# Fourier mixing and gated convolution FFN on one core: the tables loaded by halves of x, first halves of the products during the loading

## The chip, the cores and the metric

The kernel runs on one core of a Trainium2 chip. The core has five engines with instruction streams of their own: TensorE (PE, with PEld for its weight loads), VectorE (DVE), ScalarE (ACT), GpSimd (POOL) and SyncE (SP), and 16 DMA engines that serve all queues of the core. The metric is device time in microseconds (us), the median of several runs; less is better.

## The reference

`x` has 8 batches of 3136 rows and 256 features. The kernel computes the real part of a two-dimensional Fourier transform over rows and features and feeds it to a gated FFN with a convolution over the rows (`d_ff` 1024, three taps).

```python
X = np.fft.fft(x, axis=1)
X = np.fft.fft(X, axis=2)
x = X.real.astype(np.float32)
h = np.maximum(x @ w_in, 0.0)
...
for k in range(K):
    conv_out += conv_w[k][None, None, :] * hp[:, k:k + S, :]
gate = 1.0 / (1.0 + np.exp(-conv_out))
return (h * gate @ w_out).astype(np.float32)
```

## The kernel before

The transform is folded by its symmetries. Rows of x that mirror each other, and features that mirror each other, are added and subtracted on DVE (`fold_ops`, L142 to 237), so that a batch becomes two weight tiles `w`: `wt[b][0]` for the even rows of the spectrum and `wt[b][1]` for the odd ones, each with four sums (with the cosine and the sine of the features) for four residues `q` of the row. A batch is loaded in two tiles `xh[b, h]` (`load_ops`, L110 to 140): one plain DMA of 98 partitions for the lower rows, four indirect DMAs by GpSimd for the mirrored ones, and for the half `h = 1` three DMAs that bring row 0 into partition 98. Half `h` serves the residues `q = 2h` and `q = 2h + 1` of every weight tile. A tile that is loaded with `held` is first touched by a memset of GpSimd (L118), behind the issue of the loads before it.

PE multiplies the weight tiles with tables of cosines and sines (`tabs`, L242): `tab2` holds the even table (sine or cosine, four residues `q`, 393 columns each), `tab4` the odd one (four variants, of which ACT makes two from the other two, `mirror_tables`, L298; 196 columns). `load_even` (L256) brings `tab2` in four DMAs: even and odd partitions up to 95, two more rows, and the row of partition 98; `load_odd` (L270) brings one variant of `tab4` in three or four. `mend_row` (L292) scales the table rows of partitions 96 and 97. For batch 0 the odd weight tile is also scaled by `turn` factors on ACT (`scaled`, L211, operation L218), a half at a time, into tiles `h`.

The products of a batch are nine units (`Unit`, L305): `odd_even(1)`, `odd(1)`, `even_even(1)`, `even(1)`, `feature()`, then `odd_even(0)`, `odd(0)`, `even_even(0)`, `even(0)`. The argument says cosine or sine. `odd` and `odd_even` give the odd columns of the results, `even` and `even_even` the even ones; the products of `odd` and of both even units read `tab2`, those of `odd_even` read `tab4`. Each unit fills one PSUM bank by matmuls (all through `mm`, L93), ACT copies a part of the bank (`copy`) and DVE makes sums and differences of it (`fin`) that end in the result tiles `pt` (cosine) and `qt` (sine), tile `PQ[b]`. `feature` gives the row `er` of one single feature, by ten sums on GpSimd and `flip` on ACT (L460).

The main loop takes a batch in 32 steps (4 chunks of rows times 8 blocks of `d_ff`). A step makes its first product from `pt`, `qt` and the matrix `G` (`products`, L781 and L782): first `pb` from `qt`, then `pa` from `pt`, the latter on top of a seed that ACT writes from `eb` (the broadcast of `er`) and `ge` (L769). `G` and `ge` come from `w_in` and the transform matrix `dm` of the features: `blocks(i)` (L735, one fourth of the columns, four matmuls of 256 columns, two copies of ACT) and `column(i)` (L746). The weights `w_in` and `w_out` arrive as 64-bit floats and are made 32-bit by DVE (`narrow`, L606 to 639, the first step at L620). Everything else of the loop overlaps: while the steps of one batch run, the units of the next one are laid between them at fixed places. The order within each engine is the order of the program (`manual_schedule`, L66).

The change touches the start, before the first step. There the order of the program is: load of the taps (ACT's queue) and of `w_in[0]` (SP), x of batch 0 (first half on SP and GpSimd, `turn` on ACT's queue, second half on SP and GpSimd with its zero rows on ACT's queue), first use of the sigmoid (L717, which loads ACT's table of functions), narrowing of the taps and of `w_in[0]`, `taps` (L696), three memsets of GpSimd at L722 to 724 that the table loads wait for, the tables, `dm`, the other three fourths of `w_in`. Then come all folds of batch 0 (L885 to 889), eight matmuls whose result nobody reads (`keep_on`, L875, on `wt[0][1]`), mending and mirroring of the tables on ACT, and the four odd units by quarters (L898 to 908):

```python
for i in range(4):
    for j, u in enumerate(odds):
        u.part(i)
        if i == 3:
            u.copy()
            u.fin()
```

After them the units `feature`, `even_even(1)`, `even(1)`, `even_even(0)`, `even(0)` run one after the other (L910), then the broadcast of `er` by a matmul with `one` (L921), `column(0)`, the load of x's next half, `blocks(0)`, the narrowing of `w_in[1]` (L929), and the steps.

Of the kernel before, what the change touches and what calls it, by code (L numbers as in the profile page):

```python
# [9 lines left out]
F32 = mybir.dt.float32  # L10
# [27 lines left out]
def kernel(  # L38
# [71 lines left out]
    def load_ops(b, h, eng, other=None, held=False):  # L110


        def plain():
            t = xp.tile([P, 8, 2, D], F32, name="xh", tag="xh")
            xh[b, h] = t
            if held:

                nc.gpsimd.memset(t[0:1, 0, 0, 0:1], 0.0)  # L118
# [137 lines left out]
    def load_even():  # L256

        to = tabs[0].rearrange("p s q i -> p s (q i)")
        n = HQ * HE
        for i in range(2):  # L260
            nc.sync.dma_start(out=to[i:2 * MR:2], in_=dft_seq[0:MR, 0:2, HQ * i:HQ * (i + 1)]
                              .rearrange("p s q i -> p s (q i)"))
        nc.sync.dma_start(out=to[2 * MR:NP], in_=bass.AP(
            tensor=dft_seq.tensor, offset=dft_seq.offset + MR * 4 * NQ * HE,
            ap=[[n, 2], [NQ * HE, 2], [1, n]]))
        nc.sync.dma_start(out=to[NP:KR], in_=bass.AP(
            tensor=dft_seq.tensor, offset=dft_seq.offset + (NP * 4 * NQ - HQ + 2) * HE,
            ap=[[n, 1], [NQ * HE, 2], [1, n]]))

    def load_odd(eng, s):  # L270

        def at_(p, q):
            return dft_seq.offset + ((p * 4 + 2 + s) * NQ + q) * HE
        for i in range(2):
            eng.dma_start(out=tabs[1][i:2 * MR:2, s], in_=bass.AP(
                tensor=dft_seq.tensor, offset=at_(0, HQ * i + 1), ap=[[4 * NQ * HE, MR], [2 * HE, 2], [1, QO]]))
        eng.dma_start(out=tabs[1][2 * MR:NP, s], in_=bass.AP(
            tensor=dft_seq.tensor, offset=at_(MR, 1), ap=[[HQ * HE, 2], [2 * HE, 2], [1, QO]]))
        if s:
            eng.dma_start(out=tabs[1][NP:KR, 0:2, 1], in_=bass.AP(  # L280
                tensor=dft_seq.tensor, offset=dft_seq.offset + ((NP * 4 + 2) * NQ + 1) * HE,
                ap=[[HE, 1], [NQ * HE, 2], [1, QO]]))
# [15 lines left out]
    def mirror_tables():  # L298

        for to, of, s in ((2, 1, -1.0), (3, 0, 1.0)):  # L300
            for i in range(2):
                act(tabs[1][0:KR, to, :, i:QO:2], tabs[1][0:KR, of, :, i:QO:2], AF.Copy,
                    scale=-s if i else s)

    class Unit:  # L305
# [31 lines left out]
    def units(b):  # L337
# [5 lines left out]
        def even_even(sn):  # L343
# [3 lines left out]
                           True, True) for j, q in ((0, 3), (1, 1)) for c in range(2)]  # L347
# [42 lines left out]
        def odd(sn):  # L390
# [16 lines left out]
            def fin(p):  # L407
# [301 lines left out]
    w_cv.load(nc.scalar)  # L709
    w_in[0].load(nc.sync)  # L710
# [414 lines left out]
```

## Time and profile before

| | |
|---|---|
| median of 3 runs | 1173.87 us (1173.63 to 1175.4) |
| profiled execution | 1175.2 us; span 1173.4 us, granted clock 0.998 |
| PE busy | 1139.6 us (97%), 4818 matmul records |
| PEld, DVE, ACT, POOL busy | 887.5, 970.7, 942.9, 606.9 us (76, 83, 80, 52%) |
| DMA | 168.15 MB, mean 143 GB/s |
| chain that ended last | PE 77%, ACT 4%, DVE 3% |

Times in views of the profile are in us from the start of the span. A row of a timeline gives start, duration, engine, line, operation, result and operands with partitions and elements, the number of instructions (xcount), and in brackets the idle time ahead of it with what released it. SPq and ACTq are the queues' issuing instructions on those engines. q0 is the DMA queue that GpSimd fills, q1 the one of SP and ACT; their rows give packets, MB and the share of the 16 DMA engines' time in the window.

### The profile page before, as it was taken

What the parts mean: (1) busy time and instruction counts of PE and PEld (TensorE: products, weight loads), DVE (VectorE), ACT (ScalarE), POOL (GpSimd) and SP (SyncE); (2) the same over time, 40 slices, a digit from 0 to 9 for tenths busy, and PEclk for the clock granted to TensorE, in tenths of its full rate; (3) what the DMA queues carried; (4) which work ended last, traced back from release to release, by engine and by line L of the source; (5) the groups of instructions that cost most, each with busy time, mean ns of one, the idle gap of its engine ahead of it and who ended that gap; (6) DMA issues with size and microseconds to landing.
All of it is one profiled execution on the core that took longest, in us unless ns stands there. A gap on an engine that the chain in (4) does not pass through costs nothing.

```text
span 1173.4 us, 15901 instructions
## 1 busy us (share of the span) xinstructions
PE 1139.6 (97%) x4818; PEld 887.5 (76%) x4818; DVE 970.7 (83%) x1448; ACT 942.9 (80%) x1939; POOL 606.9 (52%) x734
## 2 busy tenths in 40 slices
PE   4889999999999999999999999999999999999998
PEld 2756777778778777777777777777778777777777
DVE  7589979998788789798886888889787778788885
ACT  2578868888788888888887878888887888898885
POOL 5346755666465554756455464654344344444443
PEclk9999999999999999999999999999999999999999
DMA  8777787776677676667676676865665656666654
GB/s 209 192 108 156 165 138 165 160 162 135 141 159 168 136 169 141 147 135 176 144 166 139 122 149 141 177 126 121 135 120 107 126 122 142 130 130 129 126 116 102
DMA packets 106050, 168.15 MB, mean 143 GB/s; under 512 B 31121, under 2 KB 61091, under 8 KB 105965
## 3 DMA queue, kind: packets, MB, share of 16 engines
q0 software_dynamic: 41984, 115.83, 51.7%
q1 hardware_dynamic: 62809, 50.88, 15.8%
q8 instruction: 38, 0.62, 0.2%
q10 hardware_dynamic: 1172, 0.43, 0.2%
q14 instruction: 47, 0.39, 0.1%
HBM read 38.40 MB, written 25.74 MB: 55 GB/s over the span
## 4 chain that ended last, share of the span: by engine, by line
PE 77%; ACT 4%; DVE 3%; issue 1%; DMA 0%; POOL 0%; ACTq 0%; DVEq 0%
PE po L93 49%; PE pb L93 12%; PE pa L93 11%; PE pd L93 6%; ACT nb L790 1%; DVE g L813 1%; ACT os L861 1%; ACT g L828 1%; DMA out_dram<-os 0%; ACT pa L769 0%; DVE g L837 0%; DVE w L228 0%; DVE xh L168 0%; ACT g L804 0%; DVE pt L418 0%
## 5 line engine op out<-in xcount | busy, mean ns | idle before, releaser
L93 PE MATMUL po<-wout,g 128*128 128x256 f32 x3072 | 708.3, 380 | 6.6 <-DVE g L837 5.8
L93 PEld LDWEIGHTS po<-wout,g 128*128 128x128 f32 x3072 | 581.6, 190 | 152.5 <-issue 19.7
L808 POOL DMA_DIRECT2D g<-h x256 | 227.7, 889 | 464.5 <-ACT g L804 270.6
L828 ACT ACTIVATE g<-g,cw 128x385 f32<-128x385 f32 (+2 forms) x512 | 292.3, 625 | 68.1 <-DVE g L813 65.5
L836 POOL TENSOR_TENSOR g<-g,h 128x385 f32<-128x385 f32 (+1 forms) x256 | 301.2, 1177 | 49.5 <-ACT g L828 47.9
L790 ACT ACTIVATE nb<-pb 128x386 f32<-128x386 f32 (+3 forms) x512 | 227.3, 499 | 112.1 <-PE pb L93 111.4
L798 DVE CUSTOM_DVE_ANT_0 h<-pa,nb 128x386 f32<-128x386 f32 (+3 forms) x512 | 264.3, 556 | 29.3 <-POOL h L775 19.8
L813 DVE SCALAR_TENSOR_TENSOR g<-h,cw,g 128x770 f32<-128x770 f32 (+1 forms) x256 | 282.8, 1105 | 0.0
L804 ACT ACTIVATE g<-h,cw 128x770 f32<-128x770 f32 (+1 forms) x256 | 244.4, 955 | 0.0
L93 PE MATMUL pb<-qt,G 127*128 127x387 f32 (+2 forms) x512 | 214.0, 499 | 2.6 <-ACT nb L790 1.1
L93 PE MATMUL pa<-pt,G 128*128 128x387 f32 (+2 forms) x512 | 212.3, 495 | 1.2 <-ACT pa L769 1.2
L837 DVE TENSOR_TENSOR g<-g,h 128x385 f32<-128x385 f32 (+1 forms) x256 | 187.0, 730 | 25.0 <-ACT g L828 24.8
L769 ACT ACTIVATE pa<-eb,ge 128x387 f32<-128x387 f32 (+2 forms) x256 | 155.4, 607 | 1.3 <-DVE h L798 1.0
L93 PEld LDWEIGHTS pa<-pt,G 128*128 128x128 f32 x512 | 96.4, 189 | 76.4 <-issue 17.4
L132 POOL DMA_INDIRECT xh<-in_x_dram,idx x64 | 91.1, 1423 | 18.5 <-issue 12.2
L93 PE MATMUL pd<-tab,w 98*128 98x197 f32 (+2 forms) x448 | 98.0, 318 | 0.8 <-DVE w L228 0.7
L93 PEld LDWEIGHTS pb<-qt,G 127*128 127x128 f32 x512 | 90.8, 190 | 9.7 <-ACT nb L790 2.7
L93 PEld LDWEIGHTS pd<-tab,w 98*128 98x128 f32 (+1 forms) x448 | 81.8, 191 | 10.5 <-DVE w L228 1.0
L861 ACT COPY os<-po 128x256 f32<-128x256 f32 x196 | 57.4, 395 | 6.5 <-PE po L93 6.5
L168 DVE TENSOR_TENSOR xh<-xh 98x1024 f32<-98x1024 f32 (+1 forms) x32 | 47.4, 1482 | 0.1
L157 DVE TENSOR_TENSOR xh<-xh 98x1020 f32<-98x1020 f32 (+1 forms) x32 | 46.9, 1471 | 0.0
L385 DVE TENSOR_TENSOR as<-as,pd 128x196 f32<-128x196 f32 x14 | 5.0, 358 | 38.0 <-ACT as L381 38.0
(140 smaller groups left out, 447.7 us busy)
## 6 DMA issues: line engine op xcount, KB each, us to landing
g<-h POOLq DMA_DIRECT2D x192, 385.0 KB, 4.1
g<-h POOLq DMA_DIRECT2D x64, 416.0 KB, 4.4
out_dram<-os SPq DMA_DIRECT2D x96, 256.0 KB
xh<-in_x_dram SPq DMA_DIRECT2D x16, 784.0 KB
eb<-ed SPq DMA_DIRECT2D x16, 193.5 KB
raw<-in_moe_w_in_dram SPq DMA_DIRECT2D x4, 512.0 KB
raw<-in_moe_w_out_dram SPq DMA_DIRECT2D x1, 2048.0 KB
eb<-ed SPq DMA_DIRECT2D x8, 209.0 KB
```

Of the source, the lines that this page charges most:

```text
L93: nc.tensor.matmul(o, l, r, start=start, stop=stop, skip_group_check=True)
L132: nc.gpsimd.indirect_dma_start(out=xh[b, h][0:NP, 7 - m].rearrange("p q d -> p (q d)"), out_offset=None, in_=bass.AP(tensor=x.tensor, offs ...
L769: act(pa[s][:, 0:n], eb[b, c], AF.Copy, scale=ge[:, f:f + 1])
L790: act(nb[s][:, i, cols], p[:, cols], AF.Copy, scale=-1.0 if i else 1.0)
L798: nc.vector._custom_dve(TENSOR_ADD_SAT, out=to, in0=a[:, cols], in1=c[:, i, cols], s0=BIG, s1=0.0)
L804: act(gs[s], hs[s][:, 0:n], AF.Copy, scale=cw[:, 0, s[2]:s[2] + 1])
L808: nc.gpsimd.dma_start(out=gs[s], in_=hs[s][:, 1:1 + n], accum_op=ALU.add)
L813: stt(out=g, in0=h[:, k:k + n], scalar=cw[:, k, f:f + 1], in1=g, op0=ALU.mult, op1=ALU.add)
L828: act(gs[s][:, c], gs[s][:, c], AF.Sigmoid, scale=cw[:, 1, s[2]:s[2] + 1])
L836: gt(g[:, p], g[:, p], h[:, p], op=ALU.mult)
L837: vt(g[:, v], g[:, v], h[:, v], op=ALU.mult)
L861: nc.scalar.copy(out=osb[:, j % 2], in_=pt[:, j % 2])
```

## The change

- **Tables by halves.** `load_tables(eng, h)` brings what half `h` of x needs: 590 columns (393 of residue 2h and 197 of residue 2h + 1) of each of the two rows of `tab2`, even and odd partitions in a DMA each, and the residue's part of the two loaded variants of `tab4`, two DMAs. Of the columns left out of the load, ACT makes those of the cosines from the others (`mirror_cosines`); those of the sines are not read. The rows of partitions 96 to 98 are loaded by `rest_even`, `rest_odd` and `last_row`.
- **Queues and order.** The first half's tables are issued on SP behind x's first half; x's second half is issued by GpSimd, plain DMA and indirect ones, its zero rows by SP among the tables; `dm` stands between the tables of the two halves. The rows of partitions 96 and 97 go by ACT's queue early. The first use of the sigmoid comes right behind the load of the taps. The `held` memset and two of the three memsets ahead of the tables are gone.
- **First halves.** `part` takes halves of a unit's matmuls. `even_even` and `even` are reordered so that their first half reads residues of half 0. Between the folds of half 0 and those of half 1 the program now has the first halves of the four odd units and of three of the four small even units, `blocks(0)` (both of its pieces in one bank) and `column(0)`; they stand ahead of the mending and mirroring of half 1, of its folds and of the second halves. In the main loop blocks and columns stay.
- **The matmuls that nobody reads** are ten on the taps `cw24` instead of eight on `w`; two more of 118 and 119 columns stand behind the second halves of the first two even units.
- **GpSimd takes two sums** of batch 0: those of `odd(0)` into `pt`.

```diff
-    def load_ops(b, h, eng, other=None, held=False):
+    def load_ops(b, h, eng, other=None):
...
+    HM = HO // 2 + 1
+
+    def load_tables(eng, h):
+
+        to = tabs[0].rearrange("p s q i -> p s (q i)")
+        q0, n = 2 * h * HE, HE + HM
+        for i in range(2):
+            eng.dma_start(out=to[i:2 * MR:2, :, q0:q0 + n], in_=bass.AP(
+                tensor=dft_seq.tensor, offset=dft_seq.offset + HQ * i * HE + q0,
+                ap=[[4 * NQ * HE, MR], [NQ * HE, 2], [1, n]]))
+        for i in range(2):
+            eng.dma_start(out=tabs[1][i:2 * MR:2, 0:2, h], in_=bass.AP(
+                tensor=dft_seq.tensor, offset=dft_seq.offset + (2 * NQ + HQ * i + 2 * h + 1) * HE,
+                ap=[[4 * NQ * HE, MR], [NQ * HE, 2], [1, QO]]))
+
...
-    def mirror_tables():
-
+    def mirror_tables(h):
+
+        k = KR if h else NP
         for to, of, s in ((2, 1, -1.0), (3, 0, 1.0)):
             for i in range(2):
-                act(tabs[1][0:KR, to, :, i:QO:2], tabs[1][0:KR, of, :, i:QO:2], AF.Copy,
-                    scale=-s if i else s)
+                act(tabs[1][0:k, to, h, i:QO:2], tabs[1][0:k, of, h, i:QO:2], AF.Copy, scale=-s if i else s)
+
+    def mirror_cosines():
+
+        for q, s in ((1, -1.0), (3, 1.0)):
+            t = tabs[0][0:KR, 0, q]
+            act(t[:, HM:HE][:, ::-1], t[:, 0:HE - HM], AF.Copy, scale=s)
 
...
-        def part(self, i):
-            if i == 0:
-                self.p = spare()
-            n = len(self.mms) // 4
-            for f in self.mms[i * n:(i + 1) * n]:
+        def part(self, h, bank=spare):
+            if h == 0:
+                self.p = bank()
+            n = len(self.mms) // 2
+            for f in self.mms[h * n:(h + 1) * n]:
                 f(self.p)
 
...
-                           True, True) for j, q in ((0, 3), (1, 1)) for c in range(2)]
+                           q == 1 and c == 0, True) for j, q in ((1, 1), (0, 3)) for c in range(2)]
...
-            mms = [product((slice(0, P), slice(c, HE, 2)), w(2 * sn + c), sn, q, slice(c, HE, 2), q == 2, q == 0)
-                   for c in range(2) for q in (2, 0)]
+            mms = [product((slice(0, P), slice(c, HE, 2)), w(2 * sn + c), sn, q, slice(c, HE, 2), q + c == 0, q == 2)
+                   for q in (0, 2) for c in range(2)]
...
-                vt(t[:, 1:Q4 + 1:2], a, bb, op=ALU.add)
+                tt = vt if b or sn else gt
+                tt(t[:, 1:Q4 + 1:2], a, bb, op=ALU.add)
                 x0, x1 = (bb, a) if sn else (a, bb)
-                vt(t[:, M - 1:Q4:-2], x0, x1, op=ALU.subtract)
+                tt(t[:, M - 1:Q4:-2], x0, x1, op=ALU.subtract)
...
     w_cv.load(nc.scalar)
+    act(first_use, low, AF.Sigmoid)
     w_in[0].load(nc.sync)
     for f in load_ops(0, 0, nc.sync):
         f()
     load_turn(nc.scalar)
-    for f in load_ops(0, 1, nc.sync, nc.scalar, True):
-        f()
-
-    act(first_use, low, AF.Sigmoid)
+    rest_even(nc.scalar)
     w_cv.narrow(0, 1)
     w_in[0].narrow(0, 2)
     taps()
-    act(turn[0:NP, 2], turn[0:NP, 1], AF.Copy, scale=-1.0)
+    rest_odd(nc.scalar, 0)
+    second = load_ops(0, 1, nc.gpsimd, nc.sync)
     nc.gpsimd.memset(tabs[0][0:1, 0, 0, 0:1], 0.0)
-    nc.gpsimd.memset(tabs[1][0:1, 0:2, 0, 0:1], 0.0)
-    nc.gpsimd.memset(tabs[1][96:KR, 0:2, 0], 0.0)
-    load_even()
-    load_odd(nc.sync, 0)
-    load_odd(nc.scalar, 1)
+    second[0]()
+    load_tables(nc.sync, 0)
+    for f in second[1:]:
+        f()
     nc.sync.dma_start(out=dm, in_=dft_dim[:, :, 0:2])
+    load_tables(nc.sync, 1)
+    rest_odd(nc.sync, 1)
+    last_row(nc.sync)
...
-    idle = psb.tile([P, 512], F32, name="pb", tag="pb")
-
-    def keep_on(banks):
-
-        for p in banks:
-            mm(p.rearrange("p (s q d) -> p s q d", s=2, q=2), wt[0][1][0:NP, 1, 0], wt[0][1][0:NP, 0:2, 0:2],
-               True, True)
-
+    def bank_a():
+        return psa.tile([P, 512], F32, name="pa", tag="pa")
+
+    def bank_b():
+        return psb.tile([P, 512], F32, name="pb", tag="pb")
+
+    room = left[:, NF // 2:].rearrange("p f i -> p (f i)").bitcast(I32)
     begin, us, row, flip, store = units(0)
     begin()
 
     nc.gpsimd.memset(PQ[0][1][96:P, :], 0.0)
+    odds = [us[j] for j in (0, 1, 5, 6)]
+    evens = [us[j] for j in (2, 3, 7)]
     ops, _, pres = fold_ops(0)
-    for j, f in enumerate(ops):
-        if j in pres:
-            pres[j]()
-        f()
-
-    odds = [us[j] for j in (0, 1, 5, 6)]
-    keep_on([idle] * 6)
-
-    keep_on([psa.tile([P, 512], F32, name="pa", tag="pa") for _ in range(2)])
+    act(turn[0:NP, 2], turn[0:NP, 1], AF.Copy, scale=-1.0)
+
+    def folds(h):
+        n = len(ops) // 2
+        for j in range(n * h, n * h + n):
+            if j in pres:
+                pres[j]()
+            ops[j]()
+
+    first = bank_b()
+    for _ in range(10):
+        mm(first.rearrange("p (r d) -> p r d", r=4), cw24[:, 0], cw24.to_broadcast([3 * NF, 4, P]), True, True)
+    mirror_tables(0)
+    folds(0)
+    for u in odds:
+        u.part(0)
+    for u in evens[0:2]:
+        u.part(0, bank_a)
+    both = psd.tile([P, 512], F32, name="pd", tag="pd")
+    pieces = iter((both[:, 0:N4], both[:, N4:2 * N4]))
+    blocks(0, lambda: next(pieces))
+    column(0, bank_b)
+    evens[2].part(0, bank_b)
     mend_row(1, half)
-    mirror_tables()
+    mirror_tables(1)
+    folds(1)
     mend_row(0, half)
-    for i in range(4):
-        for j, u in enumerate(odds):
-            u.part(i)
-            if i == 3:
-                u.copy()
-                u.fin()
-                if j == 1:
-                    row()
-                    w_out = Weight(wout, moe_w_out.rearrange("(c p) o -> p c o", p=P),
-                                   lambda sh: xp.tile(sh, I32, name="raw", tag="xh"))
-                    w_out.load(nc.sync)
-
-    for i, u in enumerate(us[j] for j in (4, 2, 3, 7, 8)):
-        u.matmuls(0, 1)
+    mirror_cosines()
+    for j, u in enumerate(odds):
+        u.part(1)
         u.copy()
         u.fin()
-        if i == 0:
+        if j == 1:
+            row()
+            w_out = Weight(wout, moe_w_out.rearrange("(c p) o -> p c o", p=P),
+                           lambda sh: xp.tile(sh, I32, name="raw", tag="xh"))
+            w_out.load(nc.sync)
+
+    for i, u in enumerate((us[4], *evens, us[8])):
+        if i in (0, 4):
+            u.matmuls(0, 1)
+        else:
+            u.part(1)
+            if i < 3:
+                e = 2 * HM if i == 1 else HE
+                mm(u.p[:, e:512], dm[:, 0, 0], w4[0][:, 0, 0:512 - e], False, True)
+        u.copy()
+        u.fin()
+        if i == 2:
             flip()
             store()
             spread(0, range(1, len(chunks)))
     mm(p[:, 0:n], one, er[0][:, 0:n], True, True)
     eb[0, 0] = ebp.tile([P, HN], F32, name="eb", tag="eb")[:, 0:n]
     nc.scalar.copy(out=eb[0, 0], in_=p[:, 0:n])
-    column(0)
     for f in load_ops(1, 0, nc.sync):
         f()
-    blocks(0)
-    room = left[:, NF // 2:].rearrange("p f i -> p (f i)").bitcast(I32)
     for f in w_in[1].parts(0, 2, room):
         f()
     steps = [(b, c, f) for b in range(B) for c in range(len(chunks)) for f in range(NF)]
```

More of the change, by code (lines that the diff above doesn't have):

```diff
@@ L115, in plain @@
             xh[b, h] = t
-            if held:
-                nc.gpsimd.memset(t[0:1, 0, 0, 0:1], 0.0)
             eng.dma_start(out=t[0:NP, 0:4], in_=bass.AP(
@@ L258, in load_even, with at_, rest_even @@
+    def at_(p, q, s):
+        return dft_seq.offset + ((p * 4 + s) * NQ + q) * HE
+    def rest_even(eng):
         to = tabs[0].rearrange("p s q i -> p s (q i)")
         n = HQ * HE
[L260 to L282, printed above, removed]
+        eng.dma_start(out=to[2 * MR:NP], in_=bass.AP(
+            tensor=dft_seq.tensor, offset=at_(MR, 0, 0), ap=[[n, 2], [NQ * HE, 2], [1, n]]))
@@ new lines, in rest_odd, with last_row @@
+    def rest_odd(eng, h):
+        eng.dma_start(out=tabs[1][2 * MR:NP, 0:2, h], in_=bass.AP(
+            tensor=dft_seq.tensor, offset=at_(MR, 2 * h + 1, 2), ap=[[HQ * HE, 2], [NQ * HE, 2], [1, QO]]))
+    def last_row(eng):
+        to = tabs[0].rearrange("p s q i -> p s (q i)")
+        n = HQ * HE
+        eng.dma_start(out=to[NP:KR], in_=bass.AP(
+            tensor=dft_seq.tensor, offset=at_(NP, 2 - HQ, 0), ap=[[n, 1], [NQ * HE, 2], [1, n]]))
+        eng.dma_start(out=tabs[1][NP:KR, 0:2, 1], in_=bass.AP(
+            tensor=dft_seq.tensor, offset=at_(NP, 1, 2), ap=[[HE, 1], [NQ * HE, 2], [1, QO]]))
@@ L733, with blocks @@
     ge = const.tile([P, NF], F32, name="ge")
-    def blocks(i):
+    def blocks(i, bank=spare):
         w = w4[i]
         for g in range(2):
-            p = spare()
+            p = bank()
             for t in range(2):
@@ L744, in blocks, with column @@
             column(i)
-    def column(i):
-        w, p = w4[i], spare()
+    def column(i, bank=spare):
+        w, p = w4[i], bank()
         for m in range(NF // 4):
```

1 line of the change is left out of this document (removed).

## The prediction

> **What bounds the kernel now.** I read the windows view first, then the timeline of the first 50 us engine by engine, then the DMA queues in short windows. The windows view has, for each stretch, its length, then the busy time of PE, PEld, DVE, ACT and POOL (instructions in brackets), the granted clock, the DMA share and GB/s:
>
> ```profile
> 2.00:22.00 20.00, 5.58 (x8) 2.68 (x9) 16.01 (x32) 3.36 (x8) 13.15 (x18) 1.00 1.00 244
> 46.26:250.00 203.74, 193.53 (x797) 143.12 (x798) 184.34 (x281) 163.41 (x348) 113.81 (x139) 0.99 0.76 149
> 250.00:1173.40 923.40, 917.93 (x3890) 724.26 (x3889) 754.43 (x1105) 765.84 (x1558) 470.86 (x554) 1.00 0.66 139
> ```
>
> From 250 us on PE is busy 917.93 of 923.40 us, and the change touches nothing there. It touches the stretch before 46.26. Up to 250 us PE idles 10.2 us in small gaps that wait for DVE and ACT work of the same steps, so I count a shift of the first step as a shift of the end, one to one (bounds: none of it, all of it). From 2 to 22 us the DMA engines are full (share 1.00) at 244 GB/s. The end of the start stage on PE:
>
> ```profile
> 30.07 0.60 PE L93 MATMUL po<-tab,w 98*128 98x196 f32 x2 [1.28 <-ACT tab L302]
> ...
> 35.68 0.86 PE L93 MATMUL po<-tab,h 98*128 98x197 f32 x4
> ...
> 37.28 4.85 PE L93 MATMUL po<-tab,w 99*128 99x99 f32 x32
> 42.06 0.91 PE L93 MATMUL pd<-er,one 1*128 1x386 f32 x2
> 42.91 1.05 PE L93 MATMUL po<-dm,win 128*128 128x1 f32 x8
> 43.82 1.97 PE L93 MATMUL po<-win,dm 128*128 128x256 f32 x8
> 46.26 0.92 PE L93 MATMUL pb<-qt,G 127*128 127x386 f32 x2 [0.46 <-DVE win L620]
> 47.54 0.92 PE L93 MATMUL pa<-pt,G 128*128 128x386 f32 x2 [0.37 <-ACT pa L769]
> ```
>
> A matmul is two records here. PE works nearly without a break from the odd units (to 36.54) over feature, even units, the row broadcast, column 0 and blocks 0 to the first step. My mark is the step's second product, `pa`, at 47.54: what moves it moves the end.
>
> **The change part by part.** In the built order of the changed program the first odd product against `tab2` waits for all four even-table transfers, those of the second half too: the halves lie interleaved (590 columns of each sine and cosine row). It stands third on PE, so ten matmuls of the odd first halves, the even first halves, blocks 0 and column 0 stand behind it; ACT's mending, mirroring and second-half scalings wait behind the copies of blocks 0 and column 0. I call U the landing of the second half's even tables; all is counted from there.
>
> *U.* Up to it must land, in KB, from the shapes: first weights and taps 536, x 3136, first-half tables 2 x 221.25 + 2 x 73.5 = 589.5, short rows 28, `dm` 256 (ahead in SP's queue), second-half even tables 442.5: 4988 KB or 5.11 MB. At 244 GB/s from 2.0 us that is 22.9 us. But SP issues the second half only when the first has landed, behind a row of x that waits for the first table transfer, and behind `dm`; if x is through by then, the engines stand idle for one issue and a first byte, some 1.9 us: up to 24.8. (The first load of all was issued at 0.75, and the engines were full from 2.0 on; an issue is about 0.65.) Could the tables overtake x? SP's queue, and who gets the engines when both queues hold work:
>
> ```profile
> 0.75 0.45 SPq L654 DMA_DIRECT2D raw<-in_moe_w_in_dram  x1
> 1.25 6.38 SPq L119 DMA_DIRECT2D xh<-in_x_dram  x2
> 12.84 1.64 SPq L261 DMA_DIRECT2D tab<-dft_seq_dram  x2
> ...
> 22.14 0.67 SPq L266 DMA_DIRECT2D tab<-dft_seq_dram  x1
> ```
> ```profile
> SPq L266 <- DMA tab<-dft_seq_dram: 5.7, 1, 5.7
> ```
> ```profile
> q0 software_dynamic: 219, 0.56, 79.7%
> q1 hardware_dynamic: 53, 0.13, 17.8%
> ```
> ```profile
> q1 hardware_dynamic: 364, 0.75, 80.4%
> ```
> ```profile
> g<-h POOLq DMA_DIRECT2D x192, 385.0 KB, 4.1
> ```
> ```profile
> 11.76 0.97 POOL L132 DMA_INDIRECT xh<-in_x_dram,idx  x1 [0.30 <-issue]
> ```
>
> The third fence is 14 to 17 us: two 589.5 KB tables had been issued by 14.48 on SP's queue (q1), and yet GpSimd's queue (q0), with x's indirect loads, took 79.7%; the first table landed only at 22.1 (the wait in the second fence). The fourth is 98 to 102 us, the other way: a load of x on q1 takes 80.4%. So a queue that has the engines keeps them while it has work. The change puts x's second half on q0 right behind the indirect loads of the first, issued from about 7.5 us; the tables come into q1 at the place of x's second load, which left SP at 7.63, so x likely goes first. I take U = 23.7, between 22.9 and 24.8; the low end is tables ahead of x: the first pair's second transfer is issued at about 7.63 + 0.8 = 8.4 (0.82 each at L261), lands 4.1 later (the page's 385 KB transfers), then four SP issues of 0.65 (a row, `dm`, two tables) and 4.1 again: 19.2.
>
> [...]
>
> *From U to `pa`.* The pieces:
>
> ```profile
> 26.26 1.71 ACT L218 ACTIVATE h<-w,turn 98x256 f32<-98x256 f32 x4 [6.14 <-POOL w L200]
> 28.00 0.80 ACT L296 ACTIVATE tab<-tab,half 2x196 f32<-2x196 f32 x2
> 28.83 1.19 ACT L302 ACTIVATE tab<-tab 99x196 f32<-99x196 f32 x4
> ...
> 39.85 0.93 ACT L460 ACTIVATE er<-er 1x392 f32<-1x392 f32 x1
> ...
> 43.99 0.16 ACT L752 COPY ge<-po 128x2 f32<-128x2 f32 x1 [0.50 <-PE po L93]
> 44.97 0.37 ACT L742 COPY G<-po 128x256 f32<-128x256 f32 x1 [0.81 <-PE po L93]
> ```
> ```profile
> 38.41 0.35 DVE L415 TENSOR_TENSOR as<-po,as 128x196 f32<-128x196 f32 x1
> ...
> 42.85 0.35 DVE L355 TENSOR_TENSOR as<-as,po 128x197 f32<-128x197 f32 x1
> ...
> 44.05 0.56 DVE L369 TENSOR_TENSOR pt<-as,po 128x392 f32<-128x392 f32 x1
> 45.83 0.43 DVE L620 TENSOR_SCALAR win<-raw 128x512 int32<-128x512 int32 x1 [1.23 <-PE po L93]
> ```
> ```profile
> 40.84 0.60 POOL L447 TENSOR_TENSOR er<-as 1x196 f32<-1x196 f32 x1
> ```
> ```profile
> L836 POOL TENSOR_TENSOR g<-g,h 128x385 f32<-128x385 f32 x192 | 217.8, 1134 | 40.1 <-ACT g L828 38.7 <-PE pa L93 0.8
> ```
>
> - First halves on PE: 18 matmuls took 30.07 to 36.54, 0.36 each, so ten take 3.6. Four of the sixteen even matmuls of 4.85: 1.2. Blocks 0 1.97, plus 0.45 because its two blocks now share one bank and the second waits for the first's copy (0.37); column 0 1.0. Together 8.2.
> - ACT then: 0.16, mending 0.80, mirroring 0.9 (four of half the width; 0.6 to 1.19), three of four scalings 1.3: 3.15.
> - PE, second odd halves: 3.6.
> - Last odd product to this unit's last difference on DVE: 36.54 to 38.76 before, so 2.2.
> - The first unit's two sums into `pt`, moved to GpSimd: the nearest row is 1.13 for 385 columns. I take 1.0 each, 2.0 (1.7 to 2.3). DVE would have taken about 1.0.
> - The next even copy on ACT needs that buffer: copy 0.3, flip 0.93, copy 0.3, then DVE's last unit, 42.85 to 44.61, 1.76: 3.3. Beside it run three of four `er` sums (1.65), broadcast 0.91 and its copy, hidden by 0.3.
> - Narrowing of weight block 1 on DVE (45.83) to `pa` (47.54): 1.7.
>
> Sum 8.2 + 3.15 + 3.6 + 2.2 + 2.0 + 3.3 + 1.7 = 24.15. Before, blocks 0 and column 0 (3.0 on PE) stood in front of `pa`; now they stand further up the same chain. `pa` at 23.7 + 24.15 = 47.85, 0.3 later than 47.54; break-even is U = 23.4.
>
> *The cold start.* The eight warming matmuls ran up to the first odd product; the new ten need no x and start at 5.6.
>
> ```profile
> 17.00 8.02 PE L93 MATMUL pb<-w 98*128 98x512 f32 x12 [11.40 <-POOL w L179]
> ...
> 77.53 0.92 PE L93 MATMUL pa<-pt,G 128*128 128x387 f32 x2
> 80.41 4.49 PE L93 MATMUL po<-wout,g 128*128 128x256 f32 x12 [1.97 <-DVE g L837]
> ...
> 86.05 2.75 PE L93 MATMUL po<-wout,g 128*128 128x256 f32 x12
> ```
> ```profile
> 21.40 0.34 PEld L93 LDWEIGHTS pb<-w 98*128 98x128 f32 x1 [0.52 <-issue]
> 22.25 0.22 PEld L93 LDWEIGHTS pb<-w 98*128 98x128 f32 x1 [0.52 <-issue]
> ...
> 23.14 0.19 PEld L93 LDWEIGHTS pb<-w 98*128 98x128 f32 x1 [0.24 <-issue]
> ```
>
> After 11.4 us of idling PE ran at half pace (0.85 a record at 21.40) until 22.25, then 0.45, though the windows call the clock 1.00. After 1.97 us of idling at 78.4 the same twelve records took 4.49 instead of 2.75. Twenty records, six slow and fourteen fast, end at 5.6 + 6 x 0.85 + 14 x 0.43 = 16.7. From there to U stand two matmuls; 7 us of near idling are far over 1.97. The loss lies between 4.49 - 2.75 = 1.7 and half of 5.25, 2.6; I take 2.2, all on the path, as the 8.2 us of PE work behind U are what runs slowly.
>
> [...]
>
> *Costed at nothing.* The activation table loaded before the `turn` transfers lets DVE start folding up to 2 us sooner, and the second half's folds end ahead of 30.07, as before at the latest; they are wanted only at U + 8.2 = 31.9, so the cover is 1.8 us. Issuing x by GpSimd (one transfer more, 0.97 as for an indirect load of as many rows) delays its small copies by about 1 us, ahead of U. The two 118-column fillers (0.3 each) lie before the `er` wait. A quarter fewer table columns is in the byte sum.
>
> **Forecast.** `pa` at 47.85 + 2.2 = 50.05, 2.5 us late: span 1173.4 to 1175.9. The profiled execution took 1175.2 with its launch, the median is 1173.87; on that: 1176.4. A second cooling while PE waits for ACT, about 2 us of gaps at U + 11, may add.
>
> **The rivals.**
> - *Tables first.* q1 holds the engines as at 98 us: U = 19.2, PE idle some 2.5 us behind its warming: 47.54 to 43.35, 1169.7 (1171.9 cold). For: 80.4% at 98 us. Against: q0's rows at 14 us, and q1 runs dry between its halves. From U = 21.2 down (cold) it wins.
> - *PE stays at pace.* U = 23.7, no loss: +0.3, 1174.2. Against: the rows at 17 and 80 us.
> - *Starved and cold twice.* U = 24.8, 2.6, and 1.7 more at the second gap: 1.4 + 2.6 + 1.7 = +5.7, 1179.6. For: the table issued by 14.48 that landed at 22.1.
>
> **How the numbers follow.** Forecast 0.47 (1175.3 to 1177.5 by itself), tables first 0.22, at pace 0.15, cold twice 0.16. About 0.2% (2.35 us) is what a measurement can tell: the three runs lie 1.8 us apart. Faster by more: 0.16, from tables first. Within: at pace, the rest of tables first, the lower part of the forecast: 0.34. Slower: 0.50. Range 1170.0 to 1179.5, a tenth left out on either side.
>
> **What would show it.** The first product of the `tab2` kind on PE, and with it blocks 0, right behind the landing of the second-half even tables at 22.9 to 24.8, not before x is in; matmul records of 0.35 instead of 0.17 for some 4 us behind it; the ACT copies of `G` in front of mending and mirroring; `pa` near 50. I am wrong if that product starts by 20 us, if PE is at full pace there, or if a shift of `pa` does not reach the end.

## The result, and the profile after

The changed kernel takes 1181.41 us (median of 6, 1180.16 to 1183.06) against 1173.88 us before: a ratio of 1.0057, 95% interval 1.0045 to 1.007. It is slower, as forecast, but by some 7 us and not 2.5; 1179.5 was the upper end of the range. In the profiled executions the span is 1179.3 us against 1173.4.

The timeline of PE in the changed kernel (start, duration, what, number of records), from the start to the fourth step:

```profile
5.44 17.41 PE L93 MATMUL pb<-cw 24*128 24x512 f32 x20
22.78 1.68 PE L93 MATMUL po<-tab,w 98*128 98x196 f32 x4
25.09 2.96 PE L93 MATMUL po<-tab,h 98*128 98x197 f32 x8 [0.64 <-DMA tab<-dft_seq_dram]
27.85 1.36 PE L93 MATMUL po<-tab,w 98*128 98x196 f32 x4
29.05 1.55 PE L93 MATMUL po<-tab,h 98*128 98x197 f32 x8
...
38.11 3.00 PE L93 MATMUL po<-tab,h 98*128 98x197 f32 x8 [0.17 <-ACT h L215]
40.91 1.51 PE L93 MATMUL po<-tab,w 99*128 99x196 f32 x4
42.21 1.75 PE L93 MATMUL po<-tab,h 98*128 98x197 f32 x8
...
52.51 1.38 PE L93 MATMUL pa<-pt,G 128*128 128x386 f32 x2 [1.73 <-ACT pa L785]
...
55.40 1.63 PE L93 MATMUL pb<-qt,G 127*128 127x386 f32 x2
...
77.46 2.86 PE L93 MATMUL po<-wout,g 128*128 128x256 f32 x12 [1.46 <-DVE g L853]
```

Read the durations of the same form against each other. Eight records of an odd unit take 1.55 at pace (29.05); they take 2.96 at 25.09 and 3.00 at 38.11. PE is slow three times: up to 28.9, from about 36 to 42.6, and again from `pa` to 59.7 (1.63 for a `pb` that took 0.92 before). And the first row: the twenty records of the ten warming matmuls take 0.87 each (17.41 in all), to the end at 22.85. The third matmul behind them, the first against `tab2`, starts at 25.09 behind a table transfer: this is the prediction's U. `pa` is at 52.51 instead of 47.54 (+5.0), the first product with `w_out` at 77.46 instead of

```profile
70.23 2.86 PE L93 MATMUL po<-wout,g 128*128 128x256 f32 x12 [1.46 <-DVE g L837]
```

in the kernel before: +7.2. The windows of the changed kernel (length, busy PE, PEld, DVE, ACT, POOL, granted clock, DMA share, GB/s) show the second and third slow stretch in the clock too (0.79 and 0.82), and a steady part like before's (PE 922.97 of 929.00 us):

```profile
22.00:30.00 8.00, 7.37 (x23) 6.10 (x23) 6.98 (x9) 2.14 (x8) 1.32 (x2) 1.00 0.70 195
30.00:40.00 10.00, 8.99 (x42) 7.30 (x41) 1.69 (x3) 5.62 (x17) 1.30 (x2) 0.79 0.18 68
40.00:56.00 16.00, 13.69 (x71) 10.42 (x70) 11.07 (x27) 7.26 (x20) 8.45 (x12) 0.82 0.56 176
...
250.00:1179.00 929.00, 922.97 (x3910) 727.90 (x3908) 764.25 (x1112) 769.72 (x1565) 470.69 (x559) 1.00 0.66 139
```

SP's queue and the share of the DMA queues from 8 to 12 us (packets, MB, share):

```profile
9.31 1.62 SPq L264 DMA_DIRECT2D tab<-dft_seq_dram  x2
10.98 8.54 SPq L123 DMA_DIRECT2D xh<-in_x_dram  x3
19.56 0.63 SPq L741 DMA_DIRECT2D dm<-dft_dim_dram  x1
20.65 1.30 SPq L260 DMA_DIRECT2D tab<-dft_seq_dram  x2
```
```profile
q0 software_dynamic: 322, 0.81, 92.9%
...
q1 hardware_dynamic: 15, 0.03, 4.9%
```

q1 is SP's queue alone here; the small loads that ACT issues run in a third one, q10 (5.0% in this window). x's second half on GpSimd's queue has the engines (92.9% against 4.9%), the first half's tables land only at about 21.7, short rows of x wait for them on SP (8.54 us for three issues), and the second half's tables are issued only at 20.65. And ACT, at the place where the second halves wait for it:

```profile
32.65 0.37 ACT L758 COPY G<-pd 128x256 f32<-128x256 f32 x1 [8.50 <-PE pd L93]
34.24 0.37 ACT L758 COPY G<-pd 128x256 f32<-128x256 f32 x1 [1.22 <-PE pd L93]
35.02 0.16 ACT L768 COPY ge<-pb 128x2 f32<-128x2 f32 x1 [0.41 <-PE pb L93]
35.21 0.80 ACT L304 ACTIVATE tab<-tab,half 2x196 f32<-2x196 f32 x2
36.04 0.83 ACT L311 ACTIVATE tab<-tab 99x98 f32<-99x98 f32 x4
36.77 1.69 ACT L215 ACTIVATE h<-w,turn 98x256 f32<-98x256 f32 x4
```

ACT idles 8.50 us in front of the copies of blocks 0; mending, mirroring and scaling of half 1 stand behind them. Their data were there earlier: freed from the copies, ACT did that work from 26.3 to 30.7 (e12 below).

### The profile page after: what moved, and what is told of

It is laid out like the page before. It is cut to its first block, busy times and chain, and to the rows that moved or that the text cites. A ratio compares the mean times of both kernels' runs of the same rounds, so it can differ in the third digit from the quotient of the medians.

```text
span 1179.3 us, 15911 instructions
## 1 busy us (share of the span) xinstructions
PE 1155.3 (98%) x4826; PEld 896.1 (76%) x4826; DVE 973.4 (83%) x1446; ACT 944.0 (80%) x1945; POOL 610.4 (52%) x734
## 4 chain that ended last, share of the span: by engine, by line
PE 76%; ACT 4%; DVE 4%; issue 2%; DMA 0%; POOL 0%; ACTq 0%; DVEq 0%
PE po L93 48%; PE pb L93 12%; PE pa L93 11%; PE pd L93 6%; DVE g L829 1%; ACT nb L806 1%; ACT g L844 1%; ACT os L877 1%; DMA out_dram<-os 0%; ACT pa L785 0%; DVE g L853 0%; ACT g L820 0%; DVE h L814 0%; DVE w L225 0%; DVE xh L165 0%
## 5 line engine op out<-in xcount | busy, mean ns | idle before, releaser
L853 DVE TENSOR_TENSOR g<-g,h 128x385 f32<-128x385 f32 (+1 forms) x256 | 188.2, 735 | 25.0 <-ACT g L844 24.8
L129 POOL DMA_INDIRECT xh<-in_x_dram,idx x64 | 93.5, 1461 | 19.0 <-issue 12.1
L93 PEld LDWEIGHTS pd<-tab,w 98*128 98x128 f32 x448 | 81.7, 191 | 10.6 <-DVE w L225 1.0
```

The source lines that it names most:

```text
L93: nc.tensor.matmul(o, l, r, start=start, stop=stop, skip_group_check=True)
L129: nc.gpsimd.indirect_dma_start(out=xh[b, h][0:NP, 7 - m].rearrange("p q d -> p (q d)"), out_offset=None, in_=bass.AP(tensor=x.tensor, offs ...
L853: vt(g[:, v], g[:, v], h[:, v], op=ALU.mult)
```

## The experiments

Times are medians, ratios are to runs of the kernel before on the same chip, with the 95% interval. That kernel's median lay between 1173.73 and 1175.44 there, so runs are best compared by their ratios. "pa" is the start of the first step's second product in the profiled execution, as in the prediction: one execution of each kernel.

| kernel | pa, us | time, us | ratio (interval) |
|---|---|---|---|
| before | 47.54 | 1173.88 | |
| changed | 52.51 | 1181.41 | 1.0057 (1.0045 to 1.007) |
| e1_warm128 | 51.66 | 1180.07 | 1.0050 (1.0033 to 1.0067) |
| e2_split | 50.70 | 1180.23 | 1.0057 (1.004 to 1.0074) |
| e3_dve_sums | 52.23 | 1181.02 | 1.0057 (1.0041 to 1.0074) |
| e4_warm_split_dve | 50.84 | 1177.54 | 1.0028 (1.0017 to 1.004) |
| e5_act_order | 43.41 | 1171.33 | 0.9974 (0.9963 to 0.9986) |
| e6_x_on_sp | 56.30 | 1184.97 | 1.0093 (1.0076 to 1.011) |
| e7_before_warm24 | 53.79 | 1180.20 | 1.0049 (1.0032 to 1.0066) |
| e8_x_first_all | 47.02 (run of 1173.1) | 1177.73 | 1.0029 (1.0009 to 1.0048) |
| e9_x_on_sp_clean | 53.20 | 1182.29 | 1.0065 (1.005 to 1.0081) |
| e10_seeds_first | 42.40 | 1170.66 | 0.9965 (0.9951 to 0.9978) |
| e11_x_first | 42.64 | 1171.96 | 0.9974 (0.9962 to 0.9985) |
| e12_act_order_alone | 49.28 | 1177.40 | 1.0017 (1.0008 to 1.0026) |
| e13_narrow_early | 45.98 (run of 1172.54) | 1167.30 | 0.9932 (0.9919 to 0.9946) |

**The warming matmuls.**

```diff
-    for _ in range(10):
-        mm(first.rearrange("p (r d) -> p r d", r=4), cw24[:, 0], cw24.to_broadcast([3 * NF, 4, P]), True, True)
+    for _ in range(14):
+        mm(first.rearrange("p (t d) -> p t d", t=2), w4[0][:, 0, 0:P], w4[0], True, True)
```

> The changed kernel with other warming matmuls: fourteen on the narrowed weights w4[0] (128 partitions) instead of ten on the taps (24 partitions). In the changed kernel all twenty records of the ten took 0.85 us (5.4 to 22.9) and the first products behind them ran at half pace until 28.8. Theory A (matmuls on 24 partitions do not bring PE to pace, however long): the new ones start at about 9.3, run at 0.85 for some 5 us and at 0.43 from then on, end near 24; the first halves run at pace at once, end about 2 us earlier, pa (52.51) comes near 50.5 and the time near 1179. Rival B (PE is held back at the start by something else than the rows of the operands): 28 records at 0.85 end near 33, and pa comes ten us later.

PE's timeline of this run:

```profile
9.32 15.26 PE L93 MATMUL pb<-win 128*128 128x512 f32 x28 [3.72 <-DVE win L653]
...
25.27 1.63 PE L93 MATMUL po<-tab,h 98*128 98x197 f32 x8
...
36.46 3.00 PE L93 MATMUL po<-tab,h 98*128 98x197 f32 x8 [0.60 <-ACT h L215]
...
40.56 2.55 PE L93 MATMUL po<-tab,h 98*128 98x197 f32 x8
```

Theory A for the pace: 28 records in 15.26 us (all at 0.85 would be 23.8), and the first halves at pace at once, 1.63 instead of 2.96. But `pa` gains 0.85 and not 2: the fourteen end at 24.58 and hold the first products, and PE cools again at 36.46, behind ACT. The time cannot be told from the changed kernel's. The reverse edit, in the kernel before:

```diff
-            mm(p.rearrange("p (s q d) -> p s q d", s=2, q=2), wt[0][1][0:NP, 1, 0], wt[0][1][0:NP, 0:2, 0:2],
+            mm(p.rearrange("p (s q d) -> p s q d", s=2, q=2), wt[0][1][0:24, 1, 0], wt[0][1][0:24, 0:2, 0:2],
```

> The kernel before, with its eight warming matmuls on the first 24 partitions of the same operands instead of all 98, at the same place (they start at 17.0). Theory A (rows of the operands decide whether PE comes to pace): all sixteen records take 0.85 us, they end at 30.7 instead of 26.3, the odd units behind them start at half pace and pa comes 2 to 3 us later, the time near 1176 to 1177. Rival B: records of 0.43 from 22.25 on as before, and the time within 0.5 us of before.

```profile
17.02 10.57 PE L93 MATMUL pb<-w 24*128 24x512 f32 x12 [10.96 <-POOL w L179]
27.39 3.62 PE L93 MATMUL pa<-w 24*128 24x512 f32 x4
...
31.75 1.52 PE L93 MATMUL po<-tab,h 98*128 98x197 f32 x4
...
38.82 0.86 PE L93 MATMUL po<-tab,h 98*128 98x197 f32 x4
...
53.79 0.92 PE L93 MATMUL pa<-pt,G 128*128 128x386 f32 x2 [0.37 <-issue]
```

Sixteen records, none at pace in 14 us, where 98 partitions came to it after 5.25; behind them the odd products at 1.52 instead of 0.86 for another 7 us. `pa` is 6.25 later where 2 to 3 were expected, and the time goes up by 0.49%. This one edit, 24 partitions instead of 98, costs the old kernel nearly as much as the whole change. In the changed kernel the reverse edit alone (e1) gave nothing that can be told in the time.

**The wait for the second half's tables.** `tab2` in two tiles, so that the halves no longer lie interleaved:

```diff
-    tabs = [const.tile([P, 2, HQ, HE], F32, name="tab2"), const.tile([P, 4, 2, QO], F32, name="tab4")]
+    evs = [const.tile([P, 2, 2, HE], F32, name="tab2%d" % i) for i in range(2)]
+    tabs = [None, const.tile([P, 4, 2, QO], F32, name="tab4")]
...
-            return tabs[0][0:k, st, q, cols]
+            return evs[q // 2][0:k, st, q % 2, cols]
...
```

> The changed kernel with tab2 as two tiles, one for each half of x, so that a product of the first half no longer waits for the tables of the second. Theory A (the wait for the second half's tables is on the path): the first odd product starts at about 23.9, when ACT has scaled its weights, instead of 25.09, and pa comes about 1.1 us earlier, at 51.4. Rival C (the first half's tables or ACT's mirroring and scaling end last anyway, or the second wait, on ACT, takes it over): pa moves by less than 0.3.

The first odd product starts at 24.23 instead of 25.09, and `pa` at 50.70, 1.8 earlier; the span is 1177.4 instead of 1179.3. Theory A in the profile, where the wait for the transfer is gone; but the profiled execution is the fastest of its four (1179.18 to 1181.98), and the ratio, 1.0057, is the changed kernel's.

**odd(0)'s sums on GpSimd.**

```diff
-                tt = vt if b or sn else gt
+                tt = vt
```

> The changed kernel with the two sums of odd(0) into pt on DVE, as before the change. Theory A (they are on the path, 1.0 us each on GpSimd against 0.5 on DVE, and GpSimd's sums of er stand behind them): pa about 1.0 us earlier, at 51.5, the time about 1180.4. Rival C (another chain, er's sums or the narrowing, ends last): pa within 0.3 of 52.51.

By `pa` alone (52.23, 0.28 earlier) this is rival C. But in this run the odd halves ended 0.6 later, at 44.55. Counted from their end, `pa` follows after 7.7 us and not 8.55, which speaks for theory A with 0.9 us on the path; one execution each does not settle it, and the time shows nothing.

**The three together.**

> The three edits together (fourteen warming matmuls on 128 partitions, tab2 in two tiles, odd(0)'s sums on DVE). Theory A, the three terms adding: 52.51 - 2.0 - 1.1 - 1.0 = 48.4 for pa, and the time near 1176 to 1177: still not faster than before, because x's second half lands later (its folds end at 31.7 instead of 29.95) and ACT's work for the second half stands behind the copies of blocks 0 and column 0. Rival D (the cooled clock is all of it, and a PE at pace has no gap left to cool in): pa near 47 and the time near 1174 or below.

`pa` is at 50.84, not 48.4, and PE is at half pace from 36.39 to 43 as in the changed kernel. The time, 1177.54, is half a microsecond above theory A's, but in `pa` the terms do not add (1.7 earlier, not 4.1), and rival D is wrong too: the second cooling is there with a PE that was warm at 25.

**The order on ACT.** On top of the three edits, ACT's copies of blocks 0 and column 0 (`late` collects them) move behind its mending, mirroring and scaling of half 1; their matmuls stay. `even_even(0)` is computed whole, later:

```diff
-    blocks(0, lambda: next(pieces))
-    column(0, bank_b)
-    evens[2].part(0, bank_b)
+    late = []
+    blocks(0, lambda: next(pieces), late)
+    column(0, bank_b, late)
     mend_row(1, half)
     mirror_tables(1)
     folds(1)
+    for f in late:
+        f()
...
-        if i in (0, 4):
+        if i in (0, 3, 4):
             u.matmuls(0, 1)
```

> The version with three edits (128-row warming, tab2 in two tiles, odd(0)'s sums on DVE; pa at 50.84) and one more: ACT's three copies of blocks 0 and column 0 stand behind its mending, mirroring and scaling of half 1 (their matmuls stay where they were, so the two blocks no longer wait for each other's copy), and even_even(0) is computed whole, later. There the second odd halves began at 34.4 and 36.4, each behind ACT, and PE fell back to half pace from there to 43. Theory A (the order on ACT keeps PE waiting, and the waiting cools it): the second odd halves start near 31, run at 0.17 to 0.2 us a record, end near 35 instead of 43.1; then DVE's sums are the path, pa near 43 and the time near 1170, faster than before. Rival E (the second half's folds on DVE, which end at 32.3, or PE cooling all the same, take the place): pa above 47, no faster than before.

```profile
28.53 1.89 PE L93 MATMUL pd<-win,dm 128*128 128x256 f32 x8
...
31.81 1.56 PE L93 MATMUL po<-tab,h 98*128 98x197 f32 x8
33.21 0.83 PE L93 MATMUL po<-tab,w 99*128 99x196 f32 x4
33.87 1.56 PE L93 MATMUL po<-tab,h 98*128 98x197 f32 x8
...
43.41 1.42 PE L93 MATMUL pa<-pt,G 128*128 128x386 f32 x2 [1.42 <-ACT pa L791]
```

Theory A nearly to the number: the second odd halves end at 35.4, all at pace, `pa` is at 43.41, 7.4 earlier than with the three edits alone, and the kernel is faster than before, by 0.26%. The two blocks follow each other without a break now (1.89 in one row). The same edit alone, with cold warming, one `tab2` and GpSimd's sums:

> The changed kernel with ACT's order alone: the copies of blocks 0 and column 0 behind the mending, mirroring and scaling of half 1, even_even(0) whole and later; warming on 24 partitions, one tab2 and GpSimd's sums stay. Theory A (that order is the larger part of the loss): first halves at half pace until about 29 as in the changed kernel, but the second odd halves start near 34 without a wait for ACT, at pace, and end near 37.5 instead of 43.96; pa near 47 and the time near 1175, within 1 to 2 us of before. Rival I (a PE that starts cold cools again behind the order too, so the warming must be mended first): pa above 49.5 and the time above 1177.

Between the two: `pa` at 49.28, 3.2 earlier than in the changed kernel although U came 0.85 later (25.94), and 1.0017 instead of 1.0057. The first halves were slow to 32, but the second ones ran at pace (36.72 to 40.36): no second cooling, so rival I's reason falls, though its time (above 1177) fits and its `pa` nearly: PE idled 2.1 us ahead of `pa` and was slow to 55.8. The order alone gives back some two thirds of the loss.

**x's queue.** x's second half by SP ahead of the tables, as before:

> The changed kernel, with x's second half put back on SP's queue with its zero rows on ACT's, all of it ahead of the tables, as before the change. In the changed kernel the folds of half 1 began at 22.92 behind x and ended at 31.7. Theory A (tables and x share the same engines, so the order gives to one what it takes from the other): the folds end near 30, the first-half tables land near 23 instead of 21.7 and the second-half ones near 25.5; ACT's queue, not the folds, releases the second halves, so pa stays within 0.7 of 52.5. Rival F (x's late landing is on the path): pa 1.5 to 2 us earlier.

A miss of the edit: the zero rows on ACT's queue waited behind the tables, and ACT came to the taps at 21.82.

```profile
19.00 2.77 ACTq L125 DMA_DIRECT2D xh<-in_x_dram  x2
21.82 0.18 ACT L716 COPY cw<-po 128x24 f32<-128x24 f32 x1 [18.88 <-DMA tab<-dft_seq_dram]
```

Once more with the zero rows on SP:

```diff
     rest_even(nc.scalar)
+    for f in load_ops(0, 1, nc.sync, held=True):
+        f()
...
-    second = load_ops(0, 1, nc.gpsimd, nc.sync)
```

> The changed kernel with x's second half, its zero rows too, on SP's queue and GpSimd's indirect loads, all ahead of the tables as before the change. (The earlier attempt put the zero rows on ACT's queue, where they waited behind table transfers till 21.8 and held up the taps and with them the folds by ten us.) Here ACT is left free. Theory A (x and tables share the engines; ACT's queue, not the folds, releases the second halves): folds of half 1 end near 29.5 instead of 31.7, the first products start within 1 us of 22.8 and the second-half tables land near 25.5; pa within 0.7 of 52.51 and the time within 1.5 us of the changed kernel's 1181. Rival F (x's late landing by GpSimd's queue is on the path): pa 1.5 to 2 us earlier.

Theory A in `pa` (53.20) and time: half 1's folds end at 29.47 instead of 31.7, and `pa` is no earlier. The first product against `tab2` starts at 25.91 instead of 25.09, but that is not clear of scatter: with the changed kernel's order of loads it started at 25.17 in e3 and at 25.94 in e12. So it is not shown that the tables pay for x, only that x's later landing is not on the path.

**Versions that go on from there.** First x ahead of the tables, ACT's order, and the mending of the even rows behind the odd units:

> The version with ACT's order and the three edits, and x's second half loaded by SP ahead of all tables as before the change (mending and mirroring of the even rows behind the odd units, twelve warming matmuls). Theory A (with the wait and the cooling gone, the folds of x are the path): the folds end near 29 to 30, pa near 40 to 41, the time near 1167, some 0.6% faster than before. Rival G (the tables then land so late that the first halves end behind the folds, near 31): pa no earlier than with the tables first, 43 or later.

A miss, with ten runs from 1172.55 to 1184.16: in the profiled one, which is among the fastest (1173.1), the moved mending let `feature` wait to 39.26, and the zero rows on ACT's queue held the taps to 11.17 (5.64 in the changed kernel). The ten times follow the clock: 1.000 in the three from 1172.55 to 1173.34, 0.996 at 1176, 0.988 at 1184.16. Then the seeds ahead of the narrowing of `w_in[1]`:

> The version with ACT's order (pa at 43.41, PE idle 1.4 us ahead of it and at half pace until 52) and one more edit: the two seeds of the first steps stand ahead of the narrowing of w_in[1] on ACT and DVE. Theory A (an idle of about 1.4 us ahead of pa is what cools PE there): pa near 42.3, the idle ahead of it under 0.5 us, the matmuls behind it at pace, and the time 2 to 3 us below the 1171.3 of that version. Rival H (the narrowing, now later, holds up column 1 and blocks 1 by as much, and PE idles and cools there): pa earlier, the time the same within 1 us.

```profile
42.40 0.92 PE L93 MATMUL pa<-pt,G 128*128 128x386 f32 x2 [0.34 <-ACT pa L791]
45.00 1.05 PE L93 MATMUL po<-dm,win 128*128 128x1 f32 x8 [1.69 <-DVE win L652]
...
47.35 3.53 PE L93 MATMUL po<-win,dm 128*128 128x256 f32 x8
```

Rival H: `pa` is 1.0 earlier as expected, but the idle time moves behind it (1.69 for the narrowing) and PE is slow there (3.53 instead of 1.89); the ratio goes from 0.9974 to 0.9965, within the intervals.

> The version with the seeds first, and x's second half with its zero rows on SP ahead of the tables; ACT scales half 0 before it mirrors, and mends and mirrors the even tables ahead of the copies of blocks 0. Theory A (the folds of x are the path once PE keeps its pace): folds end near 29 instead of 31.4, pa 1.5 to 2.5 us earlier than with the seeds alone, the time near 1167. Rival G (the tables then land so late that the first halves end later by as much): pa no earlier.

Rival G in effect, for another reason: folds end at 28.7 and the tables' mirroring at 21.5, but the fourteen warming matmuls run to 23.7 and PE is then busy without a break to 42.3. PE's work is the path. So fewer of them, and the narrowing where DVE waited:

```diff
-    for _ in range(14):
+    for _ in range(11):
...
     folds(1)
     mend_row(0, half)
     mirror_cosines()
+    for f in w_in[1].parts(0, 2, room):
+        f()
     for f in late:
         f()
...
     seed(steps[1])
-    for f in w_in[1].parts(0, 2, room):
-        f()
     products(steps[0])
```

> The version with x first (pa at 42.64), eleven warming matmuls instead of fourteen, and the narrowing of w_in[1] ahead of the odd units' sums, in the time in which DVE waited 4.0 us for ACT's copies. Theory A (the warming matmuls, which ended at 23.7, were ahead of the first products, and column 1's wait of 1.7 us behind pa cooled PE): first products near 22, pa near 41, no idle over 1 us behind it, matmuls of the first four steps at pace, the time near 1168. Rival J (the narrowing, which writes into the tile that blocks 0 and the fillers read, pushes DVE's sums back by as much): pa no earlier than 42.3 and the time within 1 us of 1171.

1167.30 us, 0.68% faster than before: the best version. Which of its two edits gave how much was not separated. Its profiled execution is the slowest of its five (1172.54; the others 1166.89 to 1169.08). PE's first product and the windows of that execution:

```profile
23.67 1.73 PE L93 MATMUL po<-tab,w 98*128 98x196 f32 x4 [2.70 <-DMA tab<-dft_seq_dram]
```
```profile
22.00:30.00 8.00, 6.33 (x19) 6.12 (x20) 7.86 (x11) 3.13 (x12) 2.38 (x4) 0.58 0.62 185
...
40.00:56.00 16.00, 13.92 (x70) 10.41 (x69) 9.91 (x23) 11.50 (x27) 7.33 (x12) 1.00 0.76 243
56.00:100.00 44.00, 37.81 (x149) 26.27 (x149) 39.99 (x66) 34.79 (x72) 17.90 (x30) 1.00 0.78 125
```

Here the tables landed late and PE cooled ahead of them (2.70 us of idling, clock 0.58 from 22 to 30), so its `pa` says nothing of the other four. It does show the stretch behind `pa` at full clock from 40 on, though PE idled 1.73 us there, ahead of 52.54. Theory A holds in the time, not in the idle of at most 1 us; where the first products of the faster executions started was not seen.

## Why the prediction was wrong

The chain of the prediction, with what was measured beside it:

| step | predicted | measured |
|---|---|---|
| U | 23.7 (22.9 to 24.8) | 25.09 |
| U to the end of column 0 on PE, with the cold start | 8.2 + 2.2 | 9.9 (to 34.99) |
| ACT: column 0's copy, mending, mirroring, scaling | 3.15 | 3.5 (to 38.46) |
| second odd halves | 3.6 | 5.5 (to 43.96) |
| from there to `pa` | 9.2 | 8.55 |
| `pa` | 50.05 | 52.51 |
| from `pa` to the end | 0 | +0.9 in the span |

- **The built order and U.** Right in kind: the first product against `tab2` waits for the second half's tables, q0 has most of the engines' time (92.9% from 8 to 12 us; 72.0% from 12 to 16, with 30.9% for q1), and tables first did not happen. The size was short by 1.4: U came 0.3 past its upper bound.
- **The path through ACT.** Right: ACT's work behind the copies of blocks 0 stands between first and second halves. The term "ACT then: 3.15" was nearly hit; what lay in the order itself, 3.2 us of `pa` in e12 and 7.4 in e5, was priced as a chain that has to be so.
- **The tail.** GpSimd's sums took 2.0 as predicted, the narrowing to `pa` 1.7 as predicted. From the last odd product to these sums it was 1.1 and not 2.2, from them to the narrowing 3.75 and not 3.3.
- **The step that failed is the cold start**: "Twenty records, six slow and fourteen fast, end at 16.7", with 7 us of idling behind, and a loss of "1.7 ... 2.6; I take 2.2" once. The twenty were all slow and ended at 22.85. PE did not cool by idling: it never came to pace on 24 partitions (0.87 a record for 17.4 us here, 0.9 for 14 us in e7; 128 partitions in e1 did). The first loss was of the size said (2.96 - 1.55 and 1.36 - 0.83 make 1.9). But there were three: the second, behind ACT's order, 1.45 + 0.7 + 0.2 = 2.3 on the odd halves; the third, behind the idle 1.73 ahead of `pa`, 2.3 between `pa` and the first `w_out` product (7.23 - 4.97). The prediction had only named "a second cooling ... may add", and kept it out of the sum; the rival with two coolings (1179.6, chance 0.16) came nearest.
- **One to one.** Of the 7.2 at 77 us, 1.3 were made up later: the span grew by 5.9. The medians grew by 7.5: the profiled execution of before was itself 1.3 above its median, that of after 0.35 below, which the forecast's sum did not carry. So of the 5.0 us that the forecast was short, 2.5 lie ahead of `pa` (U 1.4, the second slow stretch 1.9, the other rows -0.8), 0.9 behind it, and 1.6 in the choice of the profiled executions.

How long the warming takes can be read from the wider matmuls alone: 5.25 us before (98 partitions); in e5 and e1 (128), 28 records in 14.07 and 15.26 us, at 0.85 first and 0.43 then, make an estimated 5 and 8 at 0.85, 4.1 and 6.5 us. The 24-partition ones did not get there: 17.4 us without a break, all at half pace.

Open stays what cools PE near 36: between 31.6 and 38.1 no single idle is over 1 us, but copies, `ge` and ACT are waited for (0.46, 0.34 and 0.17 us), and column 0 has matmuls of one column. That the waits go and the cooling with them is shown (e5, e12); which of them does it is not. Short windows of the changed kernel say more of when:

```profile
28.95:35.75 6.80, 6.00 (x38) 5.38 (x36) 2.70 (x5) 1.45 (x5) 1.30 (x2) 1.00 0.39 141
35.77:42.58 6.81, 6.61 (x20) 5.53 (x20) 1.60 (x5) 5.03 (x16) 0.00 (x0) 0.50 0.01 2
42.60:52.82 10.22, 7.91 (x53) 5.62 (x52) 6.99 (x18) 5.28 (x13) 6.96 (x9) 1.00 0.68 232
52.84:59.64 6.80, 6.80 (x18) 4.48 (x17) 4.16 (x9) 3.64 (x9) 1.46 (x4) 0.50 0.70 193
```

The clock is full or half, and it stays so for 6.8, 6.8, 10.2 and 6.8 us. In the kernel before, the one stretch at half clock lasts 3.4, from 80.3 to 83.8:

```profile
80.35:83.74 3.39, 3.33 (x8) 2.68 (x9) 3.39 (x8) 3.39 (x8) 1.17 (x2) 0.50 0.52 96
```

What a slow stretch costs does not follow the wait ahead of it here: 1.97 us ahead of 80.4 came with 3.4 us at half clock, 1.73 ahead of `pa` in the changed kernel with 6.8. Nor does the length of the wait alone say whether one comes: a wait of 1.73 us in e13 and one of 2.42 in e8 were followed by full clock (1.00 from 40 to 56 us in both):

```profile
52.54 0.92 PE L93 MATMUL pb<-qt,G 127*128 127x386 f32 x2 [1.73 <-ACT G L758]
```
```profile
39.26 0.88 PE L93 MATMUL pd<-tab,ea 99*1 99x197 f32 x16 [2.42 <-issue]
```

What decides it is not shown, nor why e8's clock differs from run to run.

## What to carry to other kernels

Warm PE with matmuls that use as many partitions as the work behind them (98 and 128 did it here, 24 did not, nothing between was tried), and look at the durations of their own records: here the last was as long as the first (0.87), and the eight records of the first odd unit behind them took 2.96 instead of 1.55. When products are moved ahead, ask on each engine what now stands in front of what: here three copies, on an engine that had idled 8.5 us, cost 3.2 us of the path in the changed kernel and 7.4 with the other three edits in place. A short wait of PE can cost twice, for its length and for a slow stretch behind it (1.73 us ahead of `pa` in the changed kernel, and 2.3 more behind it): look at the records and at the clock in short windows whether it did.

## What the hardware showed that was not expected

- 24 partitions instead of 98: 0.87 us a record for 17.4 us (changed kernel) and 0.9 for 14 us (e7), never faster; 98 partitions came to 0.43 in 5.25 us (before), 128 to 0.43 in an estimated 4.1 and 6.5 (e5, e1).
- The clock column called the slow start 1.00 (22 to 30 us of the changed kernel), and showed later slow stretches as 0.79, 0.82 and 0.58: a PE that is slow from the beginning is seen in the records alone.
- Behind waits of 1.42, 2.10 and 1.73 us ahead of `pa` came 6.8 us at half clock (the changed kernel; an estimated 6.7 in e5 and e12, from a clock of 0.79 over 16 us), yet 1.73 us in e13 and 2.42 in e8 cooled nothing.
- The stretches at half clock behind a PE that had been warm lasted 3.4 us in the kernel before and 6.8 us, twice, in the changed one.
